# Gated linear attention and a bilinear FFN on one core: prefix sums as 64x64 tiles from three bf16 parts, alternating state products, and a new written order

## The chip, the cores and the metric

One NeuronCore of one Trainium2 chip runs the whole program. The metric is the device time of one execution in microseconds (us). A profile of one execution gives every instruction's start and length on TensorE (PE, with its weight loads as PEld), VectorE (DVE), ScalarE (ACT), GpSimd (POOL) and the DMA queues; SP is SyncE, which only issues transfers.

## What is computed

For 4 batch rows, 8 heads, 768 steps and head size 48, a state per head is decayed and updated at each step, and read by a query. The result, as 3072 x 384, goes through a bilinear FFN.

```python
for t in range(S):
    state = alpha[:, :, t, :, None] * state + np.einsum('bhd,bhe->bhde', k[:, :, t], v[:, :, t])
    y[:, :, t] = np.einsum('bhd,bhde->bhe', q[:, :, t], state)
...
a = x @ w_a
b = x @ w_b
return (a * b @ w_out).astype(np.float32)
```

All inputs and the output are float32; w_a and w_b are 384 x 1536, w_out is 1536 x 384.

## The kernel before

**Chunks.** The work is cut into six chunks. Chunk c holds 256 steps (`s = c // 2`) of two batch rows (`u` is 0 or 1). Each partition holds two neighbouring steps of one batch row (index `r` or `rk`), so 128 partitions hold 256 steps; the two halves of the partitions (`g`, 64 each) are the sub-chunks between which the state is carried.

**The order.** `PROGRAM` (line 17) is a written list of steps: a chunk's number, then short names with their operands. A loop at the end of the kernel issues them in that order; each engine runs its own instructions in order, and semaphores join the engines. A digit at the end of a PE step is the first of eight PSUM banks; a letter is the engine (V DVE, S ACT, P POOL, Y SP as DMA queue). `*` means both batch rows, `a` or `b` behind a batch row the lower or upper four heads. `wide(i)` takes banks i and i + 1.

**The recurrence of a chunk**, by the names of the steps:

- `ld` loads alpha, k, q and v. `ln` (L554, ACT) takes logs of alpha, `l2` (L561, DVE) adds the logs of the two steps of a partition.
- The prefix sums of these logs along the partitions are a product with an upper triangular matrix of ones, cut at the sub-chunk. Chunk 0 makes them in float32 per step (`B`, L588 and L589). Chunks 1 to 5 split the pair sums into a float32r number (`H`, L596 or L598) and the remainder (`L`, L604), and `A2` (L628) multiplies both with the 128x128 matrix `utr`, one batch row at a time into one bank.
- `E` (L656, ACT) takes Exp of the sums with both signs (`beta`, `invb`); `ra` and `lv` (L635, L642) account for the second step of a partition; `mk` and `mq` (L666) scale k and q into `QKp`.
- `C` and `Ce` turn k and q on PE (chunks 0 and 1), `T` by a transposing DMA (chunks 2 to 5), into `kqT`.
- The decay of a whole sub-chunk goes to `bls` by `dk` and `de` on PE and ACT (chunks 0 and 1), or by `dr` and `dl`, two small DMAs through memory (chunks 2 to 5).
- `K` (L744) makes the state products of one half `g`: per batch row 16 matmuls of 64x64 with 48 columns, all from the same half of the rows. `K2` (L757) makes those of both halves, alternating between them, into two banks. `k` (L771 to L775, DVE) decays and adds into the states `Sm` (middle of the chunk) and `S0` (end). In chunks 4 and 5 only the first half's are needed.
- `D` (L786) makes 16 score matmuls of 64x64 with 128 columns; they are masked by `M` on DVE (L791), or by `Mc` on ACT (L795) and `Mm` on DVE (L799).
- `SB` and `SA` (the carried states) and `Y` (the scores), all at L810, sum the outputs in two banks, `X` (L845, L847) moves them to `xT`.

**The FFN of a chunk:** `a` and `b` (L864) are three matmuls each for one of 12 blocks of the inner size, `as` (ACT) moves the first out of PSUM, `pr` (L878, DVE) multiplies the two, `o` and `oc` (L886, L897) multiply with w_out, `ot` and `otc` (L901, L903) evict, `st` and `stc` store. Chunk 0's and chunk 1's first blocks are done for one batch row at a time (256 columns), the others for both (512). `W` and `Wo` load the weights; `fill` are matmuls on zeros at the start; `cz`, `cs`, `cm`, `c1`, `c2`, `ci`, `cu` make constants and zeros.

The FFN of a chunk is written among the recurrence of the next one, so that PE always has work.

Of the kernel before, what the change touches and what calls it, by code (L numbers as in the profile page):

```python
# [8 lines left out]
F32 = mybir.dt.float32  # L9
BF16 = mybir.dt.bfloat16  # L10
# [60 lines left out]
1: mk 0 V
0: b 8 * 0
1: dk * 5
0: pr 8 *; pr 10 *; pr 9 *
1: C 0 1 3; C 0 0 4
0: o 3 0 0
1: Ce 0 1 S; de *; Ce 0 0 V; K2 0 7 3; D 0 0 4; k 0 0 V; D 0 1 1; Mc 0 0; lv 1 k P; SB 0 6; M 0 1
0: o 3 1 -
1: mk 1 V
0: o 0 0 5; ot 3 S  # L80
2: ln *
1: lv 1 q V
2: ld v * P
3: ld a * P
0: o 0 1 -
1: mq 1 V
0: o 2 0 4
1: Mm 0 0 V; k 0 1 V; C 1 0 2
0: o 1 0 0
1: Ce 1 0 V; v 1 V  # L90
2: l2 * V
0: ot 0 S; o 1 1 -
2: ra 0
1: SA 0
0: ot 1 S
2: H * S
1: D 1 0 1; K 1 0 3
2: lv 0 k P
1: M 1 0; Y 0
0: o 2 1 -  # L100
1: X 0 S; C 1 1 5
0: ot 2 S
1: a 5 0 6
2: L * V
1: Ce 1 1 V
2: lv 1 k P
1: a 3 0 1; k 1 0 V; as 3 0; a 1 0 0; as 5 0; b 1 0 7; b 3 0 2; as 1 0
2: A2 1 1
1: pr 3 0
2: ra 1  # L110
3: ld k * P
1: pr 1 0; SB 1 5
2: E 1 i
1: D 1 1 3; K 1 1 2; M 1 1
2: lv 1 q P; lv 0 q P; E 1 b
1: a 11 0 0
2: A2 0 7
1: as 11 0; b 11 0 1
# [36 lines left out]
1: pr 11 1; as 3 1
0: st 1 Y
1: as 10 1; pr 3 1
2: D 1 0 3; K * 0 1; Mc 1 0; D 1 1 6; k * 0 V
1: a 6 1 0; b 7 1 2
3: ra 1  # L160
2: Mc 1 1
1: pr 7 1
5: ld a * Y
1: b 10 1 3; o 2 1 -; as 6 1
3: ra 0
0: st 0 Y
1: b 6 1 4; ot 2 S; pr 10 1
2: Mm 1 0 V; D 0 0 2; K * 1 1
3: H * V
1: pr 6 1; o 3 0 0  # L170
2: Mc 0 0; k * 1 V; Mm 1 1 V; SB 0 4; SB 1 6
3: L * V
2: D 0 1 2
3: lv 1 q P
1: o 0 0 1
2: Mc 0 1
1: o 3 1 -
2: Mm 0 0 V
4: ln *
3: A2 1 3  # L180
2: Mm 0 1 V; SA 1
3: ld v * P
4: ld v * P
2: Y 1; Y 0; X 1 V; SA 0
3: A2 0 2
2: X 0 S
3: E 0 b
1: o 0 1 -
3: lv 0 q V; E 1 b; E 0 i; mk 0 V
1: ot 3 S  # L190
# [12 lines left out]
2: b 2 * 3
3: mq 0 V
2: a 6 * 1
3: T 0
0: st 2 Y
2: as 6 *; pr 1 *
4: l2 * V; H * V; ra 1
2: as 4 *; b 4 * 2; a 11 * 0; b 6 * 6; a 0 * 4; b 8 * 1  # L210
1: o 1 0 5
4: L * V
2: pr 2 *; pr 6 *
3: v 0 V
2: as 0 *; a 8 * 3; pr 4 *; as 11 *; pr 0 *
3: mk 1 V
2: b 11 * 2; a 7 * 6; as 8 *; pr 11 *
1: o 1 1 -
2: pr 8 *
3: T 1  # L220
1: st 2 Y
3: K2 * 2 0
1: ot 1 S
3: k * 0 V
4: ld k * Y
1: st 1 Y
3: D 0 0 3
2: as 7 *
3: Mc 0 0
2: b 9 * 1  # L230
3: k * 1 V
2: a 9 * 7
5: ld k * Y
2: b 10 * 5; as 9 *; a 10 * 6; b 7 * 3; pr 9 *; as 10 *; o 0 0 0; pr 7 *; pr 10 *
3: D 1 1 6; D 1 0 1
4: lv 1 k P
# [96 lines left out]
3: st 2 Y
4: pr 1 *; as 5 *; pr 0 *
5: v 0 V
4: a 3 * 0; a 4 * 7; as 3 *
5: D 0 0 5
4: as 4 *
5: K * 0 4; M 0 0; D 1 1 2; D 1 0 0; Mc 1 1
3: o 3 0 7  # L340
5: k * 0 V; Mc 1 0
3: o 3 1 -
5: SB 1 5
3: ot 3 S
5: SB 0 3; D 0 1 0
4: b 10 * 2
3: o 0 0 7
5: M 0 1; Mm 1 0 V; Mm 1 1 V
4: b 3 * 1; b 4 * 0
3: o 0 1 -  # L350
4: pr 4 *; b 5 * 0
3: ot 0 S
5: SA 1
# [24 lines left out]
5: pr 5 *; pr 0 *; as 8 *; a 10 * 2
4: b 11 * 4
# [658 lines left out]
```

## Time and profile before

| | |
|---|---|
| three runs | 194.92, 195.91, 201.03 us (median 195.91) |
| the profiled execution | 195.05 us, of which its span (first to last instruction) 193.3 us |
| granted TensorE clock | 1.00 |
| matmuls of the FFN, busy time (L864, L886, L897) | 56.0 + 55.5, 49.5, 2.3 us |
| prefix sums L628 | 10 + 10 matmuls, 4.5 + 3.4 us |
| state products L744, L757 | 224 and 96 matmuls, 4.9 and 1.1 us |
| DMA | 29.40 MB, HBM read 25.98 MB |

Busy time on PE is that of the instructions' own lengths, and neighbouring matmuls overlap, so it says how much PE has to do only when it is read from start to start. The page's strip shows where the engines work, in 40 slices of 4.8 us:

```
PE   7989999999999999999999999999999999999993
PEld 3878875566888876644557644456655644455562
DVE  2498787988898879579787877896585525543311
ACT  4638785656859786645547775853462353431311
POOL 8999649260927003600007400000000000000000
DMA  5999999999976989999598999006950100000342
```

Of the transfers that matter below, alpha in two loads of 192 KB on SP landed in 2.7 us, k and q in such loads in 4.8 and 4.1, outputs of 192 KB in 2.9, and a 768 KB load of k on SP in 6.3 (medians from issue to landing).

### The profile page before, as it was taken

What the parts mean: (1) busy time and instruction counts of PE and PEld (TensorE: products, weight loads), DVE (VectorE), ACT (ScalarE), POOL (GpSimd) and SP (SyncE); (2) the same over time, 40 slices, a digit from 0 to 9 for tenths busy, and PEclk for the clock granted to TensorE, in tenths of its full rate; (3) what the DMA queues carried; (4) which work ended last, traced back from release to release, by engine and by line L of the source; (5) the groups of instructions that cost most, each with busy time, mean ns of one, the idle gap of its engine ahead of it and who ended that gap; (6) DMA issues with size and microseconds to landing.
All of it is one profiled execution on the core that took longest, in us unless ns stands there. A gap on an engine that the chain in (4) does not pass through costs nothing.

```text
span 193.3 us, 5977 instructions
## 1 busy us (share of the span) xinstructions
PE 187.9 (97%) x2582; PEld 117.7 (61%) x2582; DVE 132.9 (69%) x221; ACT 106.3 (55%) x197; POOL 51.4 (27%) x69
## 2 busy tenths in 40 slices
PE   7989999999999999999999999999999999999993
PEld 3878875566888876644557544656455644455562
DVE  2498787988898879579787877896585525543311
ACT  4638785656859786645547775853462353431311
POOL 8999649260927003600007400000000000000000
PEclk9999999999999999999999999999999999999999
DMA  5999999999976989999598999006950100000342
GB/s 144 268 215 226 244 244 226 261 249 266 243 211 116 187 210 303 120 272 191 110 288 194 143 227 113 0 4 79 183 127 0 44 3 0 0 0 0 131 148 93
DMA packets 57034, 29.40 MB, mean 152 GB/s; under 512 B 47560, under 2 KB 54600, under 8 KB 57008
## 3 DMA queue, kind: packets, MB, share of 16 engines
q0 software_dynamic: 19056, 15.73, 44.2%
q1 hardware_dynamic: 37808, 13.19, 31.2%
q8 instruction: 20, 0.33, 0.7%
q10 hardware_dynamic: 144, 0.10, 0.2%
q14 instruction: 6, 0.05, 0.1%
HBM read 25.98 MB, written 4.74 MB: 159 GB/s over the span
## 4 chain that ended last, share of the span: by engine, by line
PE 91%; DMA 3%; POOL 2%; ACT 1%; DVE 1%; issue 1%; POOLq 0%; DVEq 0%
PE psum L864 48%; PE psum L886 24%; PE psum L810 7%; DMA a_t<-in_alpha_dram 3%; PE psum L786 3%; PE psum L628 2%; PE psum L707 2%; PE psum L744 2%; PE psum L897 1%; PE psum L687 1%; PE psum L588 1%; PE psum L589 1%; PE psum L757 1%; POOL v_t L547 0%; ACT la L554 0%
## 5 line engine op out<-in xcount | busy, mean ns | idle before, releaser
L864 PE MATMUL psum<-xT,wb_t 128*128 128x512 bf16 (+1 forms) x270 | 56.0, 337 | 0.0
L864 PE MATMUL psum<-xT,wa_t 128*128 128x512 bf16 (+1 forms) x270 | 55.5, 337 | 0.0
L886 PE MATMUL psum<-wo_t,prod 128*128 128x384 bf16 x276 | 49.5, 326 | 0.0
L864 PEld LDWEIGHTS <-wa_t 128*128 128x128 bf16 x270 | 25.9, 98 | 19.7 <-issue 0.2
L864 PEld LDWEIGHTS <-wb_t 128*128 128x128 bf16 x270 | 25.7, 98 | 20.0 <-issue 0.6
L886 PEld LDWEIGHTS <-prod 128*128 128x128 bf16 x276 | 26.0, 98 | 18.3 <-issue 0.5
L901 ACT ACTIVATE ot<-psum 128x384 f32<-128x384 f32 (+1 forms) x20 | 9.5, 480 | 19.5 <-PE psum L886 15.8
L642 POOL TENSOR_TENSOR k_t<-k_t,a_t 128x384 f32<-128x384 f32 x8 | 9.6, 1200 | 37.3 <-DMA k_t<-in_k_dram 35.9
L795 ACT ACTIVATE m<-psum 128x1024 bf16<-128x1024 f32 x15 | 15.1, 1022 | 4.6 <-PE psum L786 4.3
L791 DVE TENSOR_TENSOR m<-psum,mask 128x1024 bf16<-128x1024 f32 x9 | 10.9, 1216 | 3.2 <-PE psum L786 3.2
L554 ACT ACTIVATE la<-a_t 128x1536 f32<-128x1536 f32 (+2 forms) x9 | 9.5, 1055 | 5.6 <-DMA a_t<-in_alpha_dram 5.5
L845 ACT ACTIVATE xT<-psum 128x768 bf16<-128x768 f32 x8 | 6.5, 810 | 8.8 <-PE psum L810 8.7
L666 DVE TENSOR_TENSOR QKp<-k_t,invb 128x768 bf16<-128x768 f32 x10 | 9.4, 951 | 2.4 <-issue 1.5
L799 DVE TENSOR_TENSOR m<-m,mask 128x1024 bf16<-128x1024 bf16 x15 | 10.7, 736 | 0.1
L810 PE MATMUL psum<-m,vx 64*64 64x128 bf16 x576 | 10.2, 217 | 0.2 <-DVE m L799 0.2
L666 DVE TENSOR_TENSOR QKp<-q_t,beta 128x768 bf16<-128x768 f32 x10 | 10.0, 998 | 0.1
L786 PE MATMUL psum<-kqT 64*64 64x128 bf16 x384 | 9.7, 219 | 0.3 <-DVE kqT L715 0.2
L810 PEld LDWEIGHTS <-vx 64*64 64x64 bf16 x576 | 8.9, 107 | 1.0 <-issue 0.8
L547 POOL DMA_DIRECT2D v_t<-in_v_dram x8 | 8.4, 1051 | 0.1
L786 PEld LDWEIGHTS <-kqT 64*64 64x64 bf16 x384 | 6.7, 106 | 2.3 <-issue 1.9
L810 PE MATMUL psum<-kqT,Sm 64*64 64x128 bf16 x144 | 7.6, 220 | 0.1
L642 POOL TENSOR_TENSOR q_t<-q_t,ra 128x384 f32<-128x384 f32 x4 | 4.1, 1026 | 13.4 <-ACT m L795 13.1
(264 smaller groups left out, 281.1 us busy)
## 6 DMA issues: line engine op xcount, KB each, us to landing
out_dram<-ot SPq DMA_DIRECT2D x23, 192.0 KB, 2.9
a_t<-in_alpha_dram POOLq DMA_DIRECT2D x3, 768.0 KB, 13.8
q_t<-in_q_dram POOLq DMA_DIRECT2D x3, 768.0 KB, 8.7
k_t<-in_k_dram POOLq DMA_DIRECT2D x2, 768.0 KB, 11.7
v_t<-in_v_dram POOLq DMA_DIRECT2D x4, 384.0 KB, 6.2
k_t<-in_k_dram SPq DMA_DIRECT2D x2, 768.0 KB, 6.3
a_t<-in_alpha_dram POOLq DMA_DIRECT2D x3, 384.0 KB, 9.1
q_t<-in_q_dram POOLq DMA_DIRECT2D x3, 384.0 KB, 13.6
```

Source lines behind the costliest of these rows:

```text
L547: eng.dma_start(out=t[:, us, hs].rearrange("p b h r d -> p (b h) (r d)"), in_=src[ch.b0 + us.start:ch.b0 + us.stop, hs, ch.s * 2 * C:(ch.s ...
L554: nc.scalar.activation(out=ch.la[:, us, hs].rearrange("p b h r d -> p (b h r d)"), in_=ch.a[:, us, hs].rearrange("p b h r d -> p (b h r d) ...
L642: eng.tensor_mul(x, x, by)
L666: eng.tensor_mul(QKp[ch.c % 2][:, u, j, :, hs, :D], src[:, u, hs].rearrange("p h r d -> p r h d"), f)
L786: nc.tensor.matmul(s2[g * HC:(g + 1) * HC, r, p, rk, :], lhsT=ch.kqT[u][rs, 1, rk, 2 * h + p, g * HC:(g + 1) * HC], rhs=queriesT(ch, u, 2 ...
L791: nc.vector.tensor_mul(m.rearrange("p r a k s -> p (r a) (k s)"), ch.s2[u, h].rearrange("p r a k s -> p (r a) (k s)"), maskn(4))
L795: nc.scalar.activation(out=m.rearrange("p r a k s -> p (r a) (k s)"), in_=ch.s2[u, h].rearrange("p r a k s -> p (r a) (k s)"), func=AF.Copy)
L799: eng.tensor_mul(x, x, maskn(4))
L810: nc.tensor.matmul(y[c * DP:(c + 1) * DP, g, j // 2 * C:(j // 2 + 1) * C], lhsT=lhsT, rhs=rhs, start=(g, c) not in begun, stop=False, skip ...
L864: nc.tensor.matmul(p, lhsT=(wa_t, wb_t)[w][:, kk, f * 128:(f + 1) * 128], rhs=ch.xT[:, kk, us, :], start=(kk == 0), stop=(kk == KT - 1))
L886: nc.tensor.matmul(op, lhsT=ch.prod[:, f, at:at + C], rhs=wo_t[:, f, :], start=(f == 0), stop=(f == NFF - 1))
L901: nc.scalar.activation(out=o_, in_=i_, func=AF.Copy)
```

## The change

- **Prefix sums, chunks 2 to 5.** `H`, `L` and two `A2` become `sw`, two `R` and one `AQ`. `l2` has a third block: `sw` copies batch row 1's sums with the two halves of the partitions exchanged, by two DMAs of 64 partitions x 1536 bytes. `top` reads the upper 16 bits of a float32 as a bf16. `R 0` subtracts that part from the sums, `R 1` the next part from the remainder; so three bf16 parts hold the whole float32. `AQ` multiplies the three parts with the 64x64 blocks of a bf16 matrix `utb`: 3 x 2 x 2 matmuls of 384 columns into two banks, batch row 0 straight and batch row 1 crosswise. Chunk 1 keeps `H`, `L` and `A2`.
- **State products.** `K2` takes the batch rows of the two halves apart and is used for both batch rows of chunk 1 and for chunk 2, as for chunk 3 before.
- **The order** is a new one throughout: the loads at the start, the constants and who makes them, banks, and the engines of some evictions, masks, casts and scalings.
- `bls` and the row in memory have their axes in another order. New steps `dkq`, `deq`, `Cq` and `Cqe` are defined and not used.

The order, before and after, at the start (the first lines of each) and around the prefix sums of chunks 2 and 3:

```diff
-0: ld a 0b Y; cm 0; cz 0 q P; cz 0 b P; c1; cs 0 m V; c1a; ld a 0a Y; ld k 0b Y; ld q 0b Y; cu; ld q 0a Y; fill 7 6; cu2 P; ld v 0 P; cus; ld a 1 P; ln 0b
-0: B 0b 5; ln 0a; ci; ld q 1 P; B 0a 0; E 0b i; E 0b b; ld k 0a Y; cz 1 b P; ld k 1 P; dk 0 3; mk 0b V; mq 0b V; E 0a b; C 0 1 4; cm 1; ld v 1 P; E 0a i
-0: mq 0a V; W b 0 256; fill 3 1; mk 0a V; Ce 0 1 S; C 0 0 0; v 0 V; de 0; D 0 1 6; Ce 0 0 V; K 0 0 5; k 0 0 V; W a 0 256; M 0 1; D 0 0 4; SB 0 0; ln 1; W a 256 768
-0: cz 0 v V; W b 256 768; M 0 0; B 1a 2
...
+0: c1a; cu; cm 0; c1; cz 0 b V; ci; ld a 0b Y; ld a 0a Y; ld q 0b Y; ld k 0a Y; cu2 P; ld v 0 P; ld k 0b Y; fill 6 7; cus; ld q 0a Y; cz 1 v V; ln 0b; ld a 1 P
+0: ld v 1 P; B 0b 5; ld k 1 P; ln 0a; E 0b b; ld q 1 P; B 0a 3; E 0b i; cs 0 m P; E 0a i; E 0a b; mq 0b V; cz 0 q V; mk 0b V; dk 0 0; cz 1 b V; mk 0a V; de 0
+0: C 0 1 2; cm 1; fill 2 3; mq 0a V; W a 256 768; W a 0 256; C 0 0 1; Ce 0 1 S; v 0 V; K 0 0 6; Ce 0 0 V; D 0 1 4; W b 0 256; k 0 0 V; M 0 1; ln 1; SB 0 6
+0: D 0 0 0; W b 256 768; B 1a 2; cz 0 v V
...
+0: E 1a b; E 1a i; c2 V; M 0 0; W a 768 1536; B 1b 4
...
+0: dk 1 0; mq 1a V; E 1b b; mk 1a V; W b 768 1536; E 1b i; Y 0; mk 1b V; mq 1b V; C 1 0 3; SA 0; C 1 1 1; Ce 1 0 V; v 1 S; X 0 S; de 1
...
-1: Ce 0 1 S; de *; Ce 0 0 V; K2 0 7 3; D 0 0 4; k 0 0 V; D 0 1 1; Mc 0 0; lv 1 k P; SB 0 6; M 0 1
...
-2: l2 * V
...
-2: H * S
...
-2: L * V
...
-2: A2 1 1
...
-2: A2 0 7
...
-2: D 1 0 3; K * 0 1; Mc 1 0; D 1 1 6; k * 0 V
...
-2: Mm 1 0 V; D 0 0 2; K * 1 1
...
+2: l2 * V
...
+2: sw Y
...
+2: lv 1 k P; R 0
...
+2: R 1
...
+2: AQ 6; lv 0 q P
...
+2: D 1 1 6; K2 * * 2 0
...
+3: ra 1; l2 * V
...
+3: sw Y
...
+3: R 0; ld q * Y
...
+3: R 1
...
+3: AQ 2
...
+3: D 0 0 4; K2 * * 1 2; k * 0 V
```

The end of the order:

```diff
-4: st 2 Y
-5: ot 2 V; oc 1 1 0 6; oc 1 0 1 -; otc 1 0 S; st 2 Y; oc 1 1 1 -; stc 1 0 Y; otc 1 1 S; stc 1 1 S
...
+5: oc 1 0 1 -; o 3 0 7; o 2 0 4; o 0 1 -; o 3 1 -; ot 0 V; otc 1 0 V; st 0 Y; o 2 1 -; stc 1 0 Y; ot 3 S; oc 1 1 0 7; oc 1 1 1 -; ot 2 S; st 3 Y; otc 1 1 S
+5: stc 1 1 S; st 2 Y
```

The functions:

```diff
+    utb = cst.tile([C, C], BF16, name="utb")
...
+    def const_utb(eng):
+        ENG[eng].tensor_copy(utb, ut)
...
     def cross(ch, eng):
-        ch.crossed = True
         for g in range(2):
             eng.dma_start(out=ch.l2[(1 - g) * HC:(2 - g) * HC, 2].rearrange("p h d -> p (h d)"),
                           in_=ch.l2[g * HC:(g + 1) * HC, 1].rearrange("p h d -> p (h d)"))
...
+    def top(t):
+        return t.bitcast(BF16).rearrange("p b h (d t) -> p b (h d) t", t=2)[:, :, :, 1]
+
+    def rest(ch, n):
+        name = ("lh", "ll")[n]
+        t = wk.tile([C, 2, H, D], F32R, name=name, bufs=1)
+        setattr(ch, name, t)
+        x, hi = (ch.l2[:, 0::2], top(ch.l2)[:, 0::2]) if n == 0 else (ch.lh.bitcast(F32), top(ch.lh))
+        nc.vector.tensor_sub(t.bitcast(F32).rearrange("p b h d -> p b (h d)"), x.rearrange("p b h d -> p b (h d)"), hi)
...
     def cum_quads(ch, i):
         p = wide(i)[:, :, :H * D]
         for u in range(2):
             ch.pf[u, 0, H] = p[:, u]
-        for t in (ch.lh, ch.ll):
+        for n, x in enumerate((top(ch.l2)[:, 0::2], top(ch.lh), top(ch.ll))):
             for u in range(2):
                 for g in range(2):
                     gs, to = slice(g * HC, (g + 1) * HC), slice((g ^ u) * HC, ((g ^ u) + 1) * HC)
-                    nc.tensor.matmul(p[to, u], lhsT=utr[gs, gs], rhs=t[gs, u].rearrange("p h d -> p (h d)"), start=(t is ch.lh), stop=(t is ch.ll))
+                    nc.tensor.matmul(p[to, u], lhsT=utb[gs, gs], rhs=x[gs, u], start=(n == 0), stop=(n == 2))
...
-    def state_pe_both(ch, us, t0, t1):
+    def state_pe_both(ch, us0, us1, t0, t1):
         i = ch.c % 2
-        for u in range(us.start, us.stop):
-            for g, tag in enumerate((t0, t1)):
+        pair = []
+        for g, us_, tag in ((0, us0, t0), (1, us1, t1)):
+            for u in range(us_.start, us_.stop):
                 ch.kv[u, g] = bank(tag)
-            for p in range(P2):
-                for rk in range(2):
-                    for r in range(2):
-                        for g in range(2):
-                            gs = slice(g * HC, (g + 1) * HC)
-                            e = (u * P2 + p) * D
-                            nc.tensor.matmul(ch.kv[u, g][r * DP:(r + 1) * DP, e:e + D], lhsT=QKp[i][gs, u, 1, rk, 2 * p + r, :], rhs=vxs[i][gs, u, rk, 2 * p + r, :D], start=(rk == 0), stop=(rk == 1))
+            pair.append([(u, p, rk, r) for u in range(us_.start, us_.stop) for p in range(P2) for rk in range(2) for r in range(2)])
+        for both in zip(*pair):
+            for g, (u, p, rk, r) in enumerate(both):
+                gs = slice(g * HC, (g + 1) * HC)
+                e = (u * P2 + p) * D
+                nc.tensor.matmul(ch.kv[u, g][r * DP:(r + 1) * DP, e:e + D], lhsT=QKp[i][gs, u, 1, rk, 2 * p + r, :], rhs=vxs[i][gs, u, rk, 2 * p + r, :D], start=(rk == 0), stop=(rk == 1))
```

`cum_quads` and `cross` stood in the kernel before without being called. Steps that are not shown move in the order and are otherwise the same.

More of the change, by code (lines that the diff above doesn't have):

```diff
@@ new lines @@
+2: ln *
+0: o 1 1 -
+1: v 1 V
+0: ot 0 S
+2: l2 * V
+1: K2 1 1 7 2
+0: ot 1 S
+1: SA 0; k 1 0 V; Y 0
+0: ot 3 S
+1: D 1 1 4; k 1 1 V
+2: sw Y
+1: D 1 0 6; X 0 S
+0: o 2 0 3
+1: M 1 0; b 4 0 1; a 4 0 0; M 1 1; a 3 0 7
+2: lv 0 k P
+1: as 4 0
+2: ra 1
+0: o 2 1 -
+1: a 5 0 2; pr 4 0; as 3 0; as 5 0
+2: lv 1 k P; R 0
+3: ld a * P
+1: b 3 0 6
+3: ld v * P
+2: ra 0
+1: b 5 0 7; a 2 0 0; a 1 0 2; pr 3 0; as 2 0; b 10 0 1; as 1 0
+0: ot 2 S
+2: R 1
+1: pr 5 0; b 1 0 5; b 2 0 4
+2: v 1 S
+1: a 7 0 0; pr 2 0; pr 1 0; as 7 0; SB 1 2
@@ L176 @@
+1: pr 5 1
+2: D 1 0 3; M 1 1; k * 0 V
+1: a 1 1 1; o 2 0 5
+3: ra 0
+2: Mc 1 0
+1: b 1 1 4; as 1 1; o 2 1 -
+0: st 1 Y
+1: pr 1 1
+2: Mm 1 0 V
+1: b 7 1 2; ot 2 S; o 3 0 4
+3: ld k * Y
+1: pr 7 1
+2: k * 1 V; SB 1 6
+3: R 0; ld q * Y
+2: D 0 0 2
+1: o 3 1 -
+2: SB 0 0
+1: st 2 Y
+0: st 3 Y
+2: Mc 0 0; D 0 1 2
+3: R 1
 2: Mc 0 1
-1: o 3 1 -
+1: o 0 0 5
 2: Mm 0 0 V
 4: ln *
-3: A2 1 3
-2: Mm 0 1 V; SA 1
-3: ld v * P
+2: SA 1
+3: AQ 2
+2: Mm 0 1 V
+3: v 1 V
+2: SA 0; Y 1
+3: lv 0 k P
+2: Y 0; X 1 V
@@ L210 @@
[L210 to L224, printed above, removed]
+4: l2 * V
+3: E 0 i; E 1 b
+5: ld a * P
+2: b 6 * 0; a 6 * 6
+1: ot 3 V
+3: lv 0 q V; dr
+2: a 5 * 7
+3: v 0 V
+4: sw Y
+2: as 6 *
+3: mk 0 V
+2: a 1 * 2
+3: lv 1 q V
+2: b 7 * 1
+1: ot 0 V
+2: a 7 * 4; a 9 * 6
+1: o 1 0 5
@@ new lines @@
+2: pr 6 *
+3: mq 0 V
+4: ra 1
+2: as 9 *; as 7 *; pr 7 *
+3: E 1 i
+4: R 0
+2: b 9 * 0; pr 9 *; as 5 *; b 5 * 6; a 0 * 4
+3: mk 1 V
+2: b 1 * 1; as 1 *; as 0 *
+4: ra 0
+2: a 2 * 3
+1: o 1 1 -
+4: R 1
+2: pr 1 *; a 11 * 7; b 0 * 0; pr 5 *
+1: st 3 Y
+2: a 4 * 2; pr 0 *; as 2 *
+3: mq 1 V
+2: a 8 * 4; b 2 * 1
+3: T 0
+2: as 4 *
+1: ot 1 V
+2: pr 2 *; as 11 *
+3: dl; T 1
+2: b 11 * 0; b 4 * 6; a 3 * 3; as 8 *; pr 11 *
+4: v 0 V
+2: pr 4 *
+4: ld q * Y
+3: D 0 0 4; K2 * * 1 2; k * 0 V
+2: as 3 *; b 8 * 0
@@ L336 @@
[L336 to L341, printed above, removed]
+3: D 1 1 0
+1: st 0 Y
+3: Mc 1 0
+2: o 0 0 7; pr 10 *
+3: M 1 1
+2: o 2 0 2
+4: lv 1 q P
+3: SB 1 5; SB 0 3; D 0 1 0
+2: o 2 1 -
+3: Mc 0 1
+4: lv 0 q P
+5: ld q * P
+2: o 0 1 -
+3: Mm 0 1 V; Mm 1 0 V
+2: ot 2 S
+3: Mm 0 0 V
+4: AQ 0; E 1 b
+3: SA 1; SA 0; Y 1; Y 0
+5: ld v * P
+4: lv 0 k P
+3: X 1 V
+4: E 0 i
+2: o 3 0 2
+5: ra 1; lv 1 q P
+0: cs 0 0 P
+3: X 0 V
+2: o 3 1 -
@@ new lines @@
+5: l2 * V
+3: a 0 * 6
+2: ot 3 V
+4: mk 0 V
+2: st 3 Y
+4: E 0 b; v 1 S
+3: b 0 * 4
+5: sw Y
+4: E 1 i
+3: as 0 *; a 9 * 5; as 9 *
+4: mq 0 V
+3: b 9 * 2; a 2 * 1; a 8 * 6; pr 9 *
+4: T 0
+3: a 1 * 5
+4: lv 1 k V
+3: as 1 *; b 1 * 2; pr 0 *; a 4 * 0; as 4 *; a 5 * 4
+4: dr
+3: as 5 *; b 4 * 5
+4: mk 1 V; mq 1 V
+5: R 0
+3: pr 1 *
+4: T 1
+3: pr 4 *; b 6 * 3; a 6 * 4
+2: ot 0 V
+5: v 1 S
+3: b 5 * 2; as 6 *; b 8 * 0; as 8 *
+5: ra 0
+3: pr 5 *
+4: dl
+2: st 2 Y
+4: D 0 0 4
+3: a 3 * 2
+4: Mc 0 0
@@ new lines @@
+5: ld k * Y
+3: pr 6 *
+5: v 0 V
+3: as 2 *; pr 8 *; a 7 * 7; a 11 * 6; as 3 *
+5: R 1
+3: b 2 * 5
+5: lv 1 k P; lv 0 q P
+3: b 3 * 2; pr 2 *; as 7 *; as 11 *
+4: D 1 1 3; D 0 1 0
+3: pr 3 *
+4: K * 0 5; Mc 1 1; D 1 0 6; M 0 1
+2: o 1 0 2
+4: Mc 1 0; Mm 1 1 V
+3: a 10 * 3
+4: k * 0 V
+3: b 11 * 4
+2: o 1 1 -
+3: pr 11 *
+4: Mm 0 0 V; SB 0 4
+2: ot 1 S
+5: lv 0 k P
+4: SB 1 0
+5: AQ 6
+3: as 10 *; b 10 * 2
+5: E 0 b; E 0 i
+3: b 7 * 3; o 2 0 6; pr 10 *
+5: E 1 i
+4: SA 1; Mm 1 0 V; SA 0; Y 0
+3: pr 7 *
@@ new lines @@
+4: b 4 * 2
+5: X 0 V
+4: pr 4 *; a 8 * 5; a 11 * 4
+5: b 4 * 7; a 4 * 6; as 4 *; a 11 * 2
+4: b 2 * 1; pr 2 *; as 11 *
+5: pr 4 *; a 2 * 0
+4: pr 11 *
+5: as 2 *
+4: b 8 * 4
+5: b 11 * 1; a 9 * 7
+4: b 9 * 6; as 8 *
+5: as 11 *; b 2 * 0
+4: a 9 * 3
+5: a 8 * 5
+4: pr 8 *
+5: a 1 * 2; pr 2 *; a 10 * 4; a 3 * 0; as 8 *
+4: as 9 *; pr 9 *
+5: b 8 * 3; a 0 * 5; pr 11 *; pr 8 *; b 1 * 1; b 3 * 3
+4: o 0 0 6
+5: as 9 *
+4: o 2 0 7
+5: as 1 *; as 10 *; b 9 * 2
+4: o 2 1 -
+5: b 10 * 4
+4: ot 2 S
+5: pr 1 *; pr 10 *; pr 9 *
@@ L464 @@
     vxs = [cst.tile([C, 2, 2, H, VS], BF16, name=f"vx{i}") for i in range(2)]
-    bls = [cst.tile([C, B, P2], F32, name=f"bl{i}") for i in range(2)]
+    bls = [cst.tile([C, 2, 2, P2], F32, name=f"bl{i}") for i in range(2)]
     wa_t = cst.tile([128, KT, d_ff], BF16, name="wa_t")
@@ L559, in pairs @@
         us, hs = us
+        ch.apart -= set(range(us.start, us.stop))
         x = ch.la[:, us, hs].rearrange("p b h r d -> p (b h) r d")
@@ L593, in high @@
             ch.lh = wk.tile([C, 2, H, D], F32R, name="lh", bufs=1)
[L594 removed]
+        o_, i_ = (t[:, us].rearrange("p b h d -> p (b h d)") for t in (ch.lh, ch.l2))
         if eng is nc.scalar:
```

542 lines of the change are left out of this document (209 added, 333 removed).

## The prediction

> **What bounds the kernel now.** First the page's busy times and its chain of waits by engine, to see which engine sets the time.
>
> ```profile
> PE 187.9 (97%) x2582; PEld 117.7 (61%) x2582; DVE 132.9 (69%) x221; ACT 106.3 (55%) x197; POOL 51.4 (27%) x69
> ...
> PE 91%; DMA 3%; POOL 2%; ACT 1%; DVE 1%; issue 1%; POOLq 0%; DVEq 0%
> ```
>
> The chain that ended last is TensorE for 91% of 193.3 us; the rest is the first 18 us (loads, constants) and the last 3. A busy PE could still be a slow one, so next PE's own waits:
>
> ```profile
> PE psum L571 <- DVE og L475: 1.2, 1, 1.2
> PE psum L588 <- ACT la L554: 0.2, 1, 0.2
> PE psum L810 <- DVE m L799: 0.2, 1, 0.2
> PE psum L786 <- DVE kqT L715: 0.2, 1, 0.2
> ```
>
> That is all, and the last of them is over at 22.6 us. From there PE works without a gap, the granted clock is 1.00 in every stretch, and 512 columns stream in 0.216 us from start to start. So only fewer or cheaper PE instructions, or an earlier start, shorten this kernel, and anything that makes PE wait lengthens it. Then I read what the touched steps cost PE, in its timeline, whose first column is the start (the second, a single instruction's length or that of a merged group, overlaps its neighbours, so I count from start to start):
>
> ```profile
> 71.98 0.66 PE L744 MATMUL psum<-vx,QKp 64*64 64x48 bf16 x32
> 72.58 0.66 PE L886 MATMUL psum<-wo_t,prod 128*128 128x384 bf16 x3
> ...
> 94.34 0.70 PE L757 MATMUL psum<-vx,QKp 64*64 64x48 bf16 x64
> 94.86 0.40 PE L786 MATMUL psum<-kqT 64*64 64x128 bf16 x16
> 95.20 0.82 PE L864 MATMUL psum<-xT,wb_t 128*128 128x512 bf16 x3
> ...
> 126.01 1.15 PE L886 MATMUL psum<-wo_t,prod 128*128 128x384 bf16 x6
> 127.09 0.24 PE L810 MATMUL psum<-kqT,Sm 64*64 64x128 bf16 x1
> ...
> 127.55 0.44 PE L628 MATMUL psum<-lh,utr 128*128 128x384 f32 x1
> 127.83 0.33 PE L628 MATMUL psum<-ll,utr 128*128 128x384 f32 x1
> 128.00 1.25 PE L864 MATMUL psum<-xT,wb_t 128*128 128x512 bf16 x5
> ```
>
> To see: an A2 behind 64x64 work takes 0.45 us (127.55 to 128.00). Thirty-two state products from one half of the rows take 0.60 (71.98 to 72.58), the 64 alternating ones 0.52. Six output matmuls at 0.163 are 0.98, yet L810 starts 1.08 after the first of them: a change of tile size costs 0.10. Last, VectorE and the rows that the change adds to it:
>
> ```profile
> 110.00:120.00 10.00, 10.00 (x48) 4.58 (x47) 7.59 (x13) 6.85 (x13) 0.00 (x0) 1.00 1.22 170
> 120.00:130.00 10.00, 10.00 (x161) 5.56 (x160) 9.47 (x15) 7.18 (x11) 0.00 (x0) 1.00 0.07 14
> ...
> L604 DVE TENSOR_TENSOR ll<-l,lh 128x768 fp32r<-128x768 f32 x4 | 3.9, 968 | 0.0
> L598 DVE CAST lh<-l 128x768 fp32r<-128x768 f32 x2 | 1.1, 556 | 0.0
> L596 ACT ACTIVATE lh<-l 128x768 fp32r<-128x768 f32 x2 | 1.7, 854 | 0.0
> ```
>
> The columns of the first two are PE, PEld, DVE, ACT, POOL, clock, DMA: DVE at 9.47 of 10 still left PE full.
>
> **The change, part by part.**
>
> *Prefix sums, removed.* Eight A2 of chunks 2 to 5. The chain gives 0.35 for each of the four that follow a full-size matmul and 0.54 to 0.55 for the four that follow 64x64 work; 0.10 of the latter is the change of tile size, counted below. 4 x 0.35 + 4 x 0.45 = 3.2 us.
>
> *Prefix sums, added.* Four AQ, each three parts x two batch rows x two halves = 12 matmuls of 64x64 and 384 columns. How many run at once is not in the trace for this layout. The nearest row is the scores: 16 of 128 columns on all four quadrants start at 94.86 and the next work at 95.20, 0.34 with both ends, and the chain shows 0.22 when 64x64 work is on both sides; 16 x 128 / 4 = 512 columns at 0.216 says four at once. Then an AQ is 12 x 384 / 4 = 1152 columns, 0.49 us. One at a time it is 1.94. I take 0.49: 1.9 in all, so -1.3 (up to +4.6).
>
> The Trainium skill, page "TensorEngine Tiling (Array Packing)", section "Restrictions and Gotchas", speaks against this: different row tiles cannot use one PSUM bank at the same time. By that rule the saving of 1.3 would be a loss of about 0.7 (second rival).
>
> *State products.* Chunk 2 turns two K of 32 into one K2 of 64: 2 x 0.50 (0.60 less 0.10 for the tile size) - 0.52 = -0.48. The second batch row of chunk 1 is half of that, -0.24. Chunk 3 had it. Together -0.7. K2 holds two PSUM banks until both state updates have read them.
>
> *Order of PE.* I counted changes of tile size in both programs: 52 before, 56 after (SA of chunk 0 now stands alone between two transposes, among others; every AQ stands in 64x64 work). 4 x 0.10 = +0.4.
>
> *VectorE and ScalarE.* Per chunk L (0.97) and H (0.56 on DVE in chunks 3 and 4, 0.85 on ACT in 2 and 5) give way to two R, each a 768-element subtraction like L: 8 x 0.97 - 4 x 0.97 - 2 x 0.56 = +2.8 on DVE, -1.7 on ACT. The order also moves work from ACT: between 20 and 130 us four more evictions of outputs (4 x 0.56), one xT (0.96) and one cast of v (0.39): +3.5. DVE was 91.2 of 110 us there by the ten-us windows; it will be 97.5 of 108, 90%. What hides the 6.3 is the 18.8 us in which DVE stood idle, nearly all of it for PE (products after L864: 21.1 us over the run). If that cover were gone, all of it would go onto the path (first rival). I take 0.
>
> *The crossing transfers.* Each chunk's `sw` issues two DMAs of 96 KB on SP, which wait for `l2` on DVE, and R waits for both. Behind `sw` on SP stand decay rows, transposes and stores, none due before DVE's next steps. Behind R on DVE stand products and masks, for which PE waits. Between `l2` and R the new order has, by the rows' durations, 4.6, 7.0, 5.5 and 7.1 us of PE work in chunks 2 to 5. A 192 KB store landed in 2.9 us, a 768 KB load on SP in 6.3. By the first nothing is exposed, by the second 1.7 + 0.8 = 2.5. I take 0; a size of 96 KB is nearer the first. A gain is excluded: it is a new wait.
>
> *Banks.* AQ fills two banks at once until four Exp of 0.49 have read them, A2 one at a time. If the next user of a bank comes too early, PE waits up to 2.0. I take 0, with 2.0 for the range.
>
> *The start.* SP now loads k of the upper heads fifth instead of third. A sixth load was waited for 0.3 until 8.37, so a fifth lands near 7.6, and the first transposes move from 7.71 to some 8.2; PE then still has the wait for alpha until 11.83 to absorb it. POOL's work ahead of that alpha load is as long as before (ident's 0.52 takes the place of two memsets, 0.64). The first FFN matmul waited at 18.37 behind two K and a transpose, of which one K now comes later. Bounds -0.6 and +1.0; I take 0. Two fills fewer lie in idle time. The last steps (12 L897 matmuls, eviction, a store on ACT) are the same: 0.
>
> Sum: -1.3 - 0.7 + 0.4 = -1.6, that is 193.5 for the profiled execution of 195.05 (span 193.3 and 1.75 around it). The three runs shown are 194.92, 195.91 and 201.03; the median is 0.86 above the profiled one, the lowest 0.13 below. I add 0.3 as a middle and forecast **193.8**.
>
> **The rivals.**
>
> *VectorE becomes the bound, slower.* Place: DVE's queue from 20 to 130 us. Against: 95% in one window with PE full. For: 90% as a mean means that stretches stand near 100%, and DVE's idle time may sit elsewhere than the new work. If none of the 6.3 finds idle time, 195.05 + 6.3 - 1.6 = 199.8. More than 1.6 of exposed work makes it slower at all, 5.5 slower by 2%.
>
> *AQ's tiles do not overlap.* In every four-tile group of this trace (L786, L810, L757) each half of the rows writes a bank of its own; AQ writes each bank from both halves, in different partitions. Two at a time makes an AQ 0.97: 3.9 - 3.2 - 0.7 + 0.4 = +0.4, 195.5. One at a time: 7.8 - 3.2 - 0.3 = +4.3, 199.3. For: only that no row shows this layout. Against: the halves write disjoint partitions, as the scores do.
>
> *The start gains, faster.* The chain has 6.7 us between the issue of alpha's second row and its landing; loads of half the size took 2.7. Were it 4.2, all would shift by 2.5: 191.3. Against: the same loads stand ahead of it.
>
> *Nothing of it happens:* the PE steps are in the order and on the path, so I give it no chance of its own.
>
> **How the numbers follow.** Forecast 0.66, no overlap 0.09 (of it 0.02 one at a time), VectorE 0.15, the start 0.10. A difference of 2% is about what a measurement of this kernel can tell from no change: 3.9 us. Faster by that needs the start's gain, 0.10; slower needs most of VectorE's case or the serial AQ, 0.14; the rest, 0.76, is within. The range reaches down to the forecast with a better start and some of the third rival, 191.8, and up to the waits for `sw` and banks (193.8 + 2.5 + 2.0) and part of VectorE's case, 198.4.
>
> **What would show it.** AQ's twelve matmuls in about 0.5 us from first start to next work (1.0 or 1.9 for the rival); 64 state products in 0.52 in chunk 2; PE's list of waits still under 1 us after 22 us; DVE near 90% between 20 and 130; R's wait for the crossing transfers under 1 us. Wrong would be PE waits of over 2 us on DVE or ACT, or a first FFN matmul over 1 us away from 18.4.

## The result, and the profile after

The changed kernel takes 197.2 us (median of 7 runs, 196.73 to 197.95) against 195.3 (7 runs) before: a ratio of 1.0099, 95% interval 1.0074 to 1.0125. One of the seven runs before, at 201.03, fell in the kernel's slower state and is not in the ratio. The change makes the kernel slower by 1%, where 193.8 us was forecast. The profiled execution took 197.62, its span is 195.8.

The page's busy times and its chain, as shown of before:

```profile
PE 187.1 (96%) x2612; PEld 116.8 (60%) x2612; DVE 139.4 (71%) x233; ACT 101.7 (52%) x188; POOL 50.1 (26%) x66
...
PE 82%; DVE 7%; DMA 4%; ACT 3%; issue 2%; SPq 1%; DVEq 0%; ACTq 0%
```

PE was 91% of the chain and is 82%. VectorE, DMAs and ScalarE now hold 14% between them, against 5%: the end is reached through places where PE waits. PE's own list of waits (waiter, releaser, us in total, times, longest) says where:

```profile
PE psum L881 <- ACT ot L972: 1.4, 1, 1.4
...
PE psum L881 <- DVE m L870: 1.1, 2, 0.6
PE psum L881 <- DVE Sm L842: 0.5, 1, 0.5
PE psum L857 <- ACT as__1932 L941: 0.5, 1, 0.5
PE psum L935 <- DVE prod L949: 0.3, 1, 0.3
PE psum L935 <- DVE m L862: 0.3, 1, 0.3
```

All but the one for `Sm` (at 11 us) lie between 50 and 109 us: 3.6 us where there had been none. Counted from start to start, with the refilling of PE, they are 0.44 and 1.44 before 50.5 and 56.2, 0.45 and 0.54 before 94.2 and 96.8, and 0.71 twice before 107.5 and 109.0, together 4.3. In ten-us windows (length, then the busy time of PE, PEld, DVE, ACT and POOL, the clock, the DMA share and GB/s) the same three places stand out:

```profile
50.00:60.00 10.00, 8.36 (x126) 6.40 (x125) 7.94 (x14) 6.52 (x17) 3.52 (x4) 1.00 1.15 220
...
90.00:100.00 10.00, 9.25 (x120) 4.57 (x118) 9.75 (x16) 6.42 (x10) 0.00 (x0) 1.00 0.58 96
100.00:110.00 10.00, 8.89 (x233) 5.74 (x232) 8.10 (x10) 5.72 (x10) 5.47 (x5) 1.00 0.83 200
```

In two of the three VectorE is not full either (7.94 and 8.10 of 10). Its list of waits has a new entry:

```profile
DVE lh L639 <- DMA l<-l: 3.0, 2, 1.6
```

That is `R 0` standing for the crossing transfer, once in chunk 2 and once in chunk 4. How a wait on VectorE reaches PE can be followed in the timelines of chunk 2. First VectorE's (start, length, in brackets the idle time before and what ended it):

```profile
51.46 0.43 DVE L949 TENSOR_TENSOR prod<-as__1095,psum 128x256 bf16<-128x256 bf16 x1
53.29 1.68 DVE L639 TENSOR_TENSOR lh<-l 128x768 f32<-128x768 f32 x1 [1.41 <-DMA l<-l]
54.90 0.43 DVE L949 TENSOR_TENSOR prod<-as__1110,psum 128x256 bf16<-128x256 bf16 x1
```

then ScalarE's:

```profile
53.27 0.39 ACT L941 ACTIVATE as__1135<-psum 128x256 bf16<-128x256 f32 x1 [0.19 <-PE psum L935]
55.42 0.38 ACT L941 ACTIVATE as__1140<-psum 128x256 bf16<-128x256 f32 x1 [1.77 <-DVE prod L949]
55.70 0.48 ACT L972 ACTIVATE ot<-psum 128x384 f32<-128x384 f32 x1
```

`as__1110` was ready at 51.4, but its product stands behind `R 0` in VectorE's queue and starts at 54.90. There are three buffers for `as`, so the next eviction waits on ScalarE for that product until 55.42. Behind it stands the eviction of chunk 0's last output, whose bank the carried states `SB` of chunk 1 are to use, and PE waits 1.4 us for that. Half of this delay is the wait of 1.41 us, the other half `R 0` itself: it took 1.68 us, against 0.95 in chunks 3 and 4. It starts while POOL scales q (53.16 to 54.15).

The first of PE's waits, 0.44 before 50.5, is not the transfer's. PE's and VectorE's rows there are:

```profile
50.46 0.49 PE L935 MATMUL psum<-xT,wa_t 128*128 128x256 bf16 x3 [0.27 <-DVE m L862]
...
48.06 1.21 DVE L846 TENSOR_TENSOR S<-tmp,bl 128x192 bf16<-128x192 f32 x1
49.19 2.34 DVE L862 TENSOR_TENSOR m<-psum,mask 128x1024 bf16<-128x1024 f32 x2
```

An FFN block is to use a bank that the first of the two masks still reads, and that mask starts late, behind a state update of 1.21 us. `R 0` begins to stand only at 51.9. So the waits that the transfer can have caused are 1.44, 0.45 and 0.54, together 2.4.

For chunk 4 the chain shows where `R 0`'s wait comes from (start, length, what):

```profile
81.54 0.63 SPq L700
...
82.22 0.59 SPq L700
...
82.92 0.52 SPq L628
...
83.48 5.41 DMA l<-l
...
88.99 0.96 DVE lh L639
```

SP issues the two decay rows (L700) ahead of the crossing pair (L628), though the sums were ready at 81.56, and the pair's second half then needs 5.41 us from its issue.

The steps that PE was to save are there. The AQ of chunk 5 in PE's timeline, its three groups of four, and the next work; and the alternating state products of chunk 2:

```profile
129.99 0.34 PE L649 MATMUL psum<-l,utb 64*64 64x384 bf16 x4
130.16 0.34 PE L649 MATMUL psum<-lh,utb 64*64 64x384 bf16 x4
130.34 0.34 PE L649 MATMUL psum<-ll,utb 64*64 64x384 bf16 x4
130.60 0.60 PE L935 MATMUL psum<-xT,wb_t 128*128 128x512 bf16 x2
...
69.43 0.71 PE L828 MATMUL psum<-vx,QKp 64*64 64x48 bf16 x64
69.96 0.41 PE L857 MATMUL psum<-kqT 64*64 64x128 bf16 x16
```

Four start together every 0.17 us, and the whole takes 0.61 with the change of tile size, 0.51 without (0.10 by the prediction's rows): the four tiles work at once. The 64 products take 0.53.

The third place, near 107, is of another kind. Three masks of chunk 3 (L870) took 4.06 us together:

```profile
104.84 4.06 DVE L870 TENSOR_TENSOR m<-m,mask 128x1024 bf16<-128x1024 bf16 x3 [1.87 <-ACT m L866]
```

and POOL's timeline has two scalings of q of chunk 4 beside them, released by a load:

```profile
104.53 2.41 POOL L668 TENSOR_TENSOR q_t<-q_t,ra 128x384 f32<-128x384 f32 x2 [21.94 <-DMA q_t<-in_q_dram]
```

### The profile page after: what moved, and what is told of

Its sections match the earlier page's. It is cut to its first block, busy times and chain, and to the rows that moved or that the text cites. A ratio compares the mean times of both kernels' runs of the same rounds, so it can differ in the third digit from the quotient of the medians.

```text
span 195.8 us, 6066 instructions
## 1 busy us (share of the span) xinstructions
PE 187.1 (96%) x2612; PEld 116.8 (60%) x2612; DVE 139.4 (71%) x233; ACT 101.7 (52%) x188; POOL 50.1 (26%) x66
## 4 chain that ended last, share of the span: by engine, by line
PE 82%; DVE 7%; DMA 4%; ACT 3%; issue 2%; SPq 1%; DVEq 0%; ACTq 0%
PE psum L935 42%; PE psum L957 20%; PE psum L881 6%; PE psum L857 3%; DMA l<-l 3%; PE psum L752 2%; DVE m L870 2%; PE psum L608 2%; DVE prod L949 2%; PE psum L609 1%; DMA a_t<-in_alpha_dram 1%; PE psum L815 1%; PE psum L968 1%; DVE QKp L694 1%; PE psum L828 1%
## 5 line engine op out<-in xcount | busy, mean ns | idle before, releaser
L957 PE MATMUL psum<-wo_t,prod 128*128 128x384 bf16 x276 | 50.4, 326 | 0.0
L668 POOL TENSOR_TENSOR k_t<-k_t,a_t 128x384 f32<-128x384 f32 x7 | 7.7, 1099 | 44.6 <-DMA k_t<-in_k_dram 44.6
L972 ACT ACTIVATE ot<-psum 128x384 f32<-128x384 f32 (+1 forms) x15 | 7.1, 479 | 18.6 <-PE psum L957 17.9
L870 DVE TENSOR_TENSOR m<-m,mask 128x1024 bf16<-128x1024 bf16 x15 | 12.9, 879 | 1.9 <-ACT m L866 1.9
L668 POOL TENSOR_TENSOR q_t<-q_t,ra 128x384 f32<-128x384 f32 x5 | 6.3, 1264 | 26.9 <-DMA q_t<-in_q_dram 25.1
L694 DVE TENSOR_TENSOR QKp<-q_t,beta 128x768 bf16<-128x768 f32 x10 | 9.5, 948 | 0.1
L974 DVE COPY ot<-psum 128x384 f32<-128x384 f32 (+1 forms) x10 | 5.2, 531 | 5.5 <-PE psum L957 5.5
```

The source lines that it names most:

```text
L668: eng.tensor_mul(x, x, by)
L694: eng.tensor_mul(QKp[ch.c % 2][:, u, j, :, hs, :D], src[:, u, hs].rearrange("p h r d -> p r h d"), f)
L870: eng.tensor_mul(x, x, maskn(4))
L957: nc.tensor.matmul(op, lhsT=ch.prod[:, f, at:at + C], rhs=wo_t[:, f, :], start=(f == 0), stop=(f == NFF - 1))
L972: nc.scalar.activation(out=o_, in_=i_, func=AF.Copy)
```

## The experiments

The theory with which the runs were made: PE loses about 2.9 us because `R` waits for the crossing transfer in front of work that PE needs, and 1.4 because the late masks of chunk 3 meet POOL. The 2.9 holds the 0.44 before 50.5 as well, so 2.4 is the number to hold against the runs. The rival was the one of the prediction: VectorE has too much to do. All ratios are to the kernel before, run on the same chip.

**Without the transfer (`e1_nocross`).**

```diff
-2: sw Y
...
-3: sw Y
...
-4: sw Y
...
-5: sw Y
...
-        x, hi = (ch.l2[:, 0::2], top(ch.l2)[:, 0::2]) if n == 0 else (ch.lh.bitcast(F32), top(ch.lh))
+        x, hi = (ch.l2[:, 0:2], top(ch.l2)[:, 0:2]) if n == 0 else (ch.lh.bitcast(F32), top(ch.lh))
...
-        for n, x in enumerate((top(ch.l2)[:, 0::2], top(ch.lh), top(ch.ll))):
+        for n, x in enumerate((top(ch.l2)[:, 0:2], top(ch.lh), top(ch.ll))):
```

> The changed kernel with the four crossing transfers left out: the subtractions and the products of chunks 2 to 5 read batch row 1's own sums in place of the exchanged ones, so that the exchange of the halves is left out of the computation. VectorE, ScalarE and PE do the same instructions. If the crossing transfer is what makes PE wait (VectorE stood 3.0 us for it in chunks 2 and 4, and PE 0.44 + 1.44 us near 50 to 56 and 0.45 + 0.54 near 94 to 97), the time falls by about 2.9 to 194.3. If VectorE's amount of work is what PE waits for, nothing changes: 197.2. The waits of 1.4 us near 107 to 109 stay in both.

Measured: 193.52 us, ratio 0.9898 (0.9872 to 0.9924). VectorE's work is the same; between 20 and 130 us (the order of columns is that above) the changed kernel and then this one have:

```profile
20.00:130.00 110.00, 106.50 (x1628) 68.18 (x1630) 96.39 (x161) 66.37 (x125) 30.83 (x31) 1.00 1.05 200
```

```profile
20.00:130.00 110.00, 109.53 (x1706) 70.73 (x1711) 96.40 (x165) 69.21 (x132) 32.81 (x32) 1.00 1.01 192
```

VectorE is busy 96.4 us in both, PE 106.5 and 109.5. So the rival falls: at 88% VectorE leaves PE full, and it was not the work but the wait in front of it. The run also takes eight issues off SP's queue; the next run keeps them. The gain, 0.0201 of the time or 3.9 us, is more than the 2.9 expected: no wait is left on PE after 13 us. The one before 50.5 went (the state update took 0.70 here), and so did those near 107, which neither theory had said: the masks here ran from 102.70 and took 1.90 for the three.

**The same work, later (`e2_later_r`).**

```diff
-2: lv 1 k P; R 0
+2: lv 1 k P
...
-2: R 1
 1: pr 5 0; b 1 0 5; b 2 0 4
+2: R 0; R 1
...
-4: R 0
...
-4: R 1
+4: R 0
...
+4: R 1
 3: dl; T 1
```

> The changed kernel with nothing removed, only the two subtractions moved later in the written order: in chunk 2 behind the third of the products that they stood ahead of, in chunk 4 by one place each (the first to where the second was, the second some five products later). By the transfer theory the products no longer stand behind a wait, and PE's waits near 50 to 56 and 94 to 97 shrink from 2.9 to at most 0.5: 194.3 to 194.8. By the theory that VectorE has too much work: 197.2, as its work is the same.

Measured: 194.41 us, ratio 0.9948 (0.9916 to 0.9981), 3.0 us better than the changed kernel with not one instruction fewer. What PE still waits for near 56 and 50, and VectorE in chunk 4:

```profile
PE psum L649 <- DVE ll L639: 0.5, 1, 0.5
...
PE psum L935 <- DVE m L862: 0.3, 1, 0.3
...
DVE lh L639 <- DMA l<-l: 0.5, 1, 0.5
```

The wait for the transfer fell from 3.0 to 0.5, and the waits near 94 and 97 are gone. Of the one near 56, 0.68 from start to start is left, now at AQ itself, which follows close behind `R 1`; the one near 50, which `R` had no part in, is still there with 0.43. The masks of chunk 3 took 1.90 here as well, and the 1.4 us near 107 are part of the 3.0.

**The load of q earlier (`e3_early_q`), and both (`e4_both`).**

```diff
-3: dl; T 1
+3: dl
+4: ld q * Y
+3: T 1
...
-4: ld q * Y
```

> The changed kernel with one load moved: q of chunk 4 is issued on SP ahead of chunk 3's second transpose instead of behind it. POOL's two scalings of that q then run some 5 us earlier and no longer beside the three masks of chunk 3 that took 4.06 us instead of about 2.0. If that meeting of POOL and VectorE costs PE the 0.71 + 0.71 us near 107 to 109: 195.8. If these waits come from the amount of VectorE's work or from the transfer alone: 197.2.

> The two moves together (subtractions later, q of chunk 4 earlier). If both causes are right and separate: 197.2 - 2.6 - 1.4 = 193.2, which is 1.1% under the kernel before. If PE's waits come from VectorE's amount of work: 197.2. If one wait only takes the place of the other: 194.5 to 196.

Measured: 196.1 us, ratio 1.0026 (0.9994 to 1.0058), for the load alone; 194.61, ratio 0.9952 (0.9921 to 0.9982), for both. With q early POOL's two scalings run from 97.38, the three masks took 2.20, and the waits near 107 are gone: 0.0073 of the time, 1.4 us, as expected, with the waits for the transfer still in place (3.4 us on VectorE). Near 56 PE waited only 0.5 in all here, where `R 0` stood 0.96 and took 0.96: the 1.4 of the changed kernel was made by the wait and the long subtraction together. But the two gains do not add, and 193.2 was wrong. Once the subtractions are later, everything up to the masks runs 2 us earlier and misses POOL's scalings anyway, so the second move has nothing left to remove; in its place PE waits 0.2 us for a transposing DMA of chunk 3, which now stands behind the load on SP.

**The parts of PE's work (`e6_old_sums`, `e5_k_back`, `e9_order`).** The first puts the old sums into the new order, the second the old state products into the kernel with the subtractions later, the third both old parts into the new order.

```diff
-2: lv 1 k P; R 0
+2: lv 1 k P; H * V
...
-2: R 1
+2: L * V
...
-2: AQ 6; lv 0 q P
+2: A2 0 6; A2 1 7; lv 0 q P
```

and so in chunks 3 to 5, without `sw`; and

```diff
-1: K2 1 1 7 2
+1: K 1 0 7; K 1 1 2
...
-2: D 1 1 6; K2 * * 2 0
+2: D 1 1 6; K * 0 2; K * 1 0
```

> The changed kernel, its order kept, with the prefix sums of chunks 2 to 5 as they were before: no crossing transfer, H on VectorE where the first subtraction stood, L where the second stood, two A2 where each AQ stood. PE's work grows by the 1.3 us that the new sums were to save, and VectorE's falls by about 1.6. Against the run without the crossing transfers (193.5, same order, new sums, no transfer): 194.8 if the saving of 1.3 is real, 193.5 if the tiles save nothing. Against the changed kernel (197.2): faster in either case by the theory that the transfer costs 2.9 or more.

> The kernel with the subtractions moved later (194.4), with the state products of chunk 1's second batch row and of chunk 2 as two groups of one half each again. If the alternation saves what I counted: 194.4 + 0.7 = 195.1. If these products lie beside other work: 194.4.

> The new order alone: old prefix sums and old state products in it. By the count of PE's work this is the kernel before plus 0.4 for four more changes of tile size: 195.3 to 195.7. If the new order itself loses (PE waits that come from where steps stand, without any crossing transfer): above 196.5. If it gains at the start: below 194.8.

Measured: 195.12 (ratio 0.9973, 0.9951 to 0.9995), 194.94 (0.9966, 0.9945 to 0.9987) and 195.47 (0.9999, 0.9972 to 1.0026). The new order alone shows no difference from the old one. The new sums, had they no transfer, save 0.9973 - 0.9898 = 0.0075, or 1.5 us. The alternating products save 0.9999 - 0.9973 = 0.0026 in one pair of runs and 0.9966 - 0.9948 = 0.0018 in the other, 0.4 to 0.5 us; either difference is smaller than the intervals of its two runs, so these do not show that it is above nothing. The traces do better, since in the runs without the transfer, with the old sums and with both old parts PE's list has no wait behind the first FFN matmul. These are the first FFN matmuls and the last matmuls of the three, in this order:

```profile
19.16 0.50 PE L931 MATMUL psum<-xT,wa_t 128*128 128x256 bf16 x3
...
187.83 1.15 PE L964 MATMUL psum<-wo_t,prod 128*128 128x192 bf16 x12
```

```profile
19.69 0.50 PE L931 MATMUL psum<-xT,wa_t 128*128 128x256 bf16 x3
...
190.10 0.74 PE L964 MATMUL psum<-wo_t,prod 128*128 128x192 bf16 x7
```

```profile
18.18 0.50 PE L931 MATMUL psum<-xT,wa_t 128*128 128x256 bf16 x3
...
189.11 0.74 PE L964 MATMUL psum<-wo_t,prod 128*128 128x192 bf16 x7
```

From the first to the end of the last, PE takes 169.82, 171.15 and 171.67 us: the new sums save 1.3 and the alternating products 0.5, by one execution each.

**Is it other loads that make the transfer late (`e10_loads_later`)?**

```diff
-3: ld a * P
 1: b 3 0 6
-3: ld v * P
...
 2: AQ 6; lv 0 q P
+3: ld a * P; ld v * P
```

> The changed kernel with only two loads moved: alpha (768 KB) and v (384 KB) of chunk 3 are issued on POOL behind its scaling of q of chunk 2, at about 54 us instead of 49 to 51, when chunk 2's crossing transfer has landed. If the transfer lands late (6.1 us instead of 4.2 in chunk 5) because it shares the DMA engines with those loads, it lands 1 to 2 us earlier and PE's 1.4 us near 56 go: 195.3 to 196.2. If its 6 us are its own or come from loads issued before it: 197.2.

Measured: 198.87 us, ratio 1.0159 (1.0115 to 1.0203). The transfer of chunk 2 landed in 5.3 us instead of 6.1, but `R 0` was released only 0.4 us earlier (52.93 for 53.29) and VectorE's wait there stayed at 1.46; that of chunk 4 landed in 6.5. VectorE's wait in chunk 4 grew from 1.61 to 2.73, and PE waited 0.5 us for a transposing DMA, so the time rose instead of staying at 197.2. The expectation of a gain was wrong, and those two loads are not what makes the transfer slow. What does stays open: over the runs a DMA of the pair landed in 5.3 to 6.5 us in chunks 2 and 4; in chunk 5 in 3.2 to 4.3, and once in 2.0, though the DMA engines were not at rest there (198 GB/s in the changed kernel, against 253 in chunk 2 and 216 in chunk 4). For chunk 3 the traces hold no landing.

**A version that beats both (`e7_best`, `e8_best_mended`).** The subtractions of chunk 2 two products later still, those of chunk 4 as in `e2_later_r`, AQ beside the next 64x64 work, and other banks for some FFN blocks of chunk 1. This is the second of the two; the first has `a 1 0 2` in place of `a 1 0 7`.

```diff
-1: M 1 0; b 4 0 1; a 4 0 0; M 1 1; a 3 0 7
+1: M 1 0; b 4 0 1; a 4 0 0; M 1 1; a 3 0 2
...
-1: a 5 0 2; pr 4 0; as 3 0; as 5 0
+1: a 5 0 7; pr 4 0; as 3 0; as 5 0
...
-1: b 5 0 7; a 2 0 0; a 1 0 2; pr 3 0; as 2 0; b 10 0 1; as 1 0
+1: b 5 0 2; a 2 0 0; a 1 0 7; pr 3 0; as 2 0; b 10 0 1; as 1 0
...
-1: a 7 0 0; pr 2 0; pr 1 0; as 7 0; SB 1 2
-2: AQ 6; lv 0 q P
+1: a 7 0 0; pr 2 0; pr 1 0
+2: R 0; R 1
+1: as 7 0; SB 1 2
...
+2: AQ 6
+1: SA 1; as 11 0; Y 1; b 11 0 5
+2: E 1 i; E 1 b; E 0 b
```

> The kernel with the subtractions moved later (194.4), with its two remaining waits in chunk 1 taken away: in chunk 2 the subtractions stand two products later still and AQ next to the following 64x64 work, and three FFN blocks of chunk 1 use other banks, so that none waits for the mask of the scores. PE waited 0.4 and 0.7 us there: 193.3 if they vanish, 194.4 if one wait only takes the place of another.

> The kernel with the subtractions later, AQ of chunk 2 beside the following 64x64 work, and four FFN blocks of chunk 1 in other banks (a 3 in bank 2, a 5 and a 1 in 7, b 5 in 2). The run before it with this aim put a 1 into the bank of b 5 ahead of b 5's product. PE's remaining waits of the later-subtractions kernel were 0.4 and 0.7 to 0.9 us near 50 and 56: 193.3 to 193.9, 0.8 to 1.1% under the kernel before. 194.4 if a wait takes their place.

Measured: 193.88 us for the first, ratio 0.9923 (0.9888 to 0.9958). In it `a 1 0` overwrites the bank of `b 5 0` before that block's product is made, so one block of chunk 1's inner layer is changed. The mended one takes 194.01, ratio 0.9924 (0.9897 to 0.9952), on PE's list only 0.2 us after 22 us:

```profile
PE psum L651 <- DVE ll L641: 0.2, 1, 0.2
...
DVE lh L641 <- DMA l<-l: 0.8, 1, 0.8
```

It is 0.8% under the kernel before and 1.7% under the changed one, with the change's three parts in it; that it is better than the one with the subtractions merely later (0.9948) is not shown. VectorE still stands 0.8 us for the transfer of chunk 4, but now with nothing behind it that PE needs at once.

## Why the prediction was wrong

**What bounds the kernel.** Right: PE's work from 22 us on sets the time, and what makes PE wait lengthens it. All of the loss is such waits. The prediction took 2% as the least that a measurement can tell; the interval of the result is a quarter of a per cent to each side, and the 1% is clear of it.

**Prefix sums, -1.3.** Right: 1.5 by the medians, 1.3 by the traces. An AQ takes 0.51 without its change of tile size, for 0.49, so the rival of tiles that do not overlap is dead. The Trainium skill, page "TensorEngine Tiling (Array Packing)", section "Restrictions and Gotchas", is contradicted in its short form by this trace: two row tiles wrote one bank at once, at full rate, each in partitions of its own. The Trainium skill, page "PSUM — Partial Sum Buffer", section "PSUM bank collisions raise a hardware error", quotes the same short form, but reports a measured conflict of two row tiles only for the same bank and the same 32 partitions. The 0.51 us agrees with that.

**State products, -0.7.** The right direction, too large: 0.4 to 0.5. The 64 products of chunk 2 take 0.53 as forecast. In chunk 2 the stretch from the scores to the next full-size matmul is 1.49 us with the old products and 1.13 with the new (the runs with both old parts and with the old sums), 0.36 less where 0.48 was forecast. In chunk 1 the stretch from the products to the next full-size matmul is 1.81 and 1.67, 0.14 less for 0.24. The last old products of chunk 2 start among the scores behind them (68.56 to 68.67), so the 0.50 that I gave each old group was in part shared with its neighbours.

**Order of PE, +0.4, and the start, 0.** The order alone came out at 0.9999 with an interval of a quarter of a per cent to each side (0.5 us). That allows the 0.4 but does not show it. In the profiled executions the first FFN matmul stood at 18.20 before and 18.11 after, as forecast; over the other runs it lay between 17.5 and 19.7.

**VectorE, 0, and its rival.** The work was forecast as 97.5 us between 20 and 130 us and is 96.4; that it costs nothing was right, as the run without the transfer shows. The rival at 15% was the wrong mechanism for slower.

**The crossing transfers, 0: the step that failed.** "By the first nothing is exposed, by the second 1.7 + 0.8 = 2.5. I take 0; a size of 96 KB is nearer the first." The transfers landed in 6.1 us in chunk 2, 5.4 in chunk 4 and 4.2 in chunk 5, not in the 2.9 of a store, and VectorE waited 1.4 and 1.6 us in just the two chunks that I had marked. The 2.9 was also a median over the whole run. In the stretch of chunks 3 and 4 of the same trace, from 66 to 100 us, the row of the stores reads (KB, median us to landing):

```profile
out_dram<-ot SPq DMA_DIRECT2D x8, 192.0 KB, 6.1
```

The stores of the last 15 us, which landed in 1.9 to 2.2, had pulled the median down. A transfer's size was the wrong way to choose between the rows: the 192 KB stores and the 768 KB loads differ by more than size, and the nearest in kind, a small transfer on SP that other work waits for, was the 3 KB reload of the decay at 2.8, which is no nearer. The end that the rows gave, 2.5, held the VectorE wait of 3.0 nearly; it stood in the range but not in the forecast. The prediction also put the decay rows behind `sw` on SP. In chunk 4 two of them stand ahead of it and hold SP for 1.3 us after the sums were ready; had the pair been issued then and taken as long, most of the 1.6 would not have been there. That is an estimate from the chain's rows; no run moved them. The Trainium skill, page "DMA: Bandwidth & Descriptors", section "Anatomy of one DMA — SWDGE (gpsimd) path", gives a fixed 2 us and the rest by bytes, for DMAs issued from GpSimd; an estimate by it is 2.2 us for 96 KB. The pairs here were issued on SP, and all the landings that the traces show but one, of 2.0, took 3.2 us or more.

**Who waits for it.** I had named the products behind `R`, but not how short the way from there to PE is: three `as` buffers, an eviction behind them on ScalarE, and a bank. So 3.0 us of waiting on VectorE, with 0.7 more of a long `R 0`, cost 2.4 on PE. The 0.44 before 50.5 came from the bank of a mask, a wait that the prediction does not have; the last version uses other banks there.

**What the lateness then met.** Not in the prediction at all: 1.4 us from three slow masks, two of them beside POOL's scalings. That is a consequence here, since it goes away with the transfer's wait or with an earlier load of q, and only once.

The sum by measured terms: 0.0 for the new order with its start (uncertain by 0.5), -1.3 and -0.5 for PE's work, +4.3 for its waits, is +2.5; the span of the profiled execution grew by 2.5.

## What to carry to other kernels

When a step on an in-order engine is to wait for a new transfer, price the transfer by how its likes on that queue land in the stretch where it will run, not by a median of the whole run, look at what the queue issues ahead of it, and then move the waiting step behind whatever the busiest engine needs next: that move alone, with no work removed, was worth 3.0 us here, 1.4 of them from what the lateness had met. Test a suspected overload of an engine by keeping its work and taking only the wait away; the two look alike on a profile page. And gains from removing two waits in a row don't add when the second is only the first one's lateness.

## What the runs showed of the hardware

A mask on VectorE (both inputs in SBUF, bf16) takes 0.68 us, and up to 1.50 when it starts while a tensor operation of POOL runs: so the one at 75.83 in the kernel before (1.498) and two of the three in chunk 3 of the changed one (1.229, 1.490). Each of these three ended 0.55 us after POOL's operation did, as if it had stood until then; the masks that had started before POOL's operation kept their length (0.681 at 75.23 and 0.692 at 101.27 before, both still running when POOL began). The subtraction `R 0` of chunk 2 (1.68 in place of 0.95) ended 0.82 us after POOL's scaling. The third slow mask, at 107.41, took 1.494 while POOL was listed as issuing loads; in the kernel with the subtractions later, masks beside the same issuing took 0.684. Spans on POOL are rough, so what slows that one is open.

A copy of 96 KB from one half of the partitions to the other, issued on SP, took 5.3 to 6.5 us to land in chunks 2 and 4 and, but for one of 2.0, 3.2 to 4.3 in chunk 5. Beside the landings of chunk 4 that is nothing special: the six 192 KB stores issued on SP between 73 and 105 us of the changed kernel whose landing is recorded took 3.7 to 7.0.
